# Attention with a gated feed-forward on one core: another hand-written order of TensorE's work, with longer runs of value blocks and the maxima's transpositions inside them

## The chip, the cores and the metric

One NeuronCore of a Trainium2 chip runs the whole program. The metric is the device time of one execution in microseconds (us), as the median of several runs; lower is better. A second source is one profiled execution, whose trace gives every instruction's engine, start and duration. TensorE is called PE here, VectorE DVE, ScalarE ACT, GpSimd POOL and SyncE, which issues most DMAs, SP.

## The reference

A layer norm, a 32-head attention of head width 16 over 2048 tokens, and a SwiGLU feed-forward that gates the attention's output; everything in float32.

```python
def reference(A_x, A_wqkv, A_wo, B_x, B_w1, B_w3, B_w2):
    x = A_x                                    # [1, 2048, 512]
    xn = _layernorm(x, axis=-1)
    s = _A_ref(xn, A_wqkv, A_wo)               # softmax(q k^T / 4) v, 32 heads of 16, then @ wo
    g = _silu(_B_ref(xn, B_w1, B_w3, B_w2))    # (silu(xn w1) * (xn w3)) w2, F = 1792
    return x + s * g
```

## The kernel before

A prologue of about 159 us normalises x, projects it to q, k and v (split into a high and a low part, so that single-pass float32r products keep the precision) and starts on the maxima of the first scores. Then one long main part runs two things at once on PE: the attention, phase by phase (32 phases: 16 pairs of heads times two halves of the queries), and the feed-forward. A tail adds the output projection.

PE's work in the main part consists of four kinds of pieces:

- **Half products** use 64 of the array's 128 rows, so two of them, one on rows 0 to 63 and one on rows 64 to 127, can run side by side. The code calls these two the lanes 0 and 1. There are three sorts: scores (`e`, line 627, one per head of the pair), products for the maxima (`m`, line 389, the scores of a later phase with queries on the partitions, of which only the row maximum is kept), and products of the feed-forward (`f`, line 858).
- **Value blocks** (`pv`, line 640): four matmuls that multiply one tile of keys' exponentials with the values. They use all 128 rows and a quarter of the columns each, and add up in one PSUM bank that belongs to them.
- **Transpositions** of the negated maxima (`m<-ident,nm`, line 404), one a phase. What they give goes by ACT and DVE (`mh`, `ml`) and four small DMAs on SP (line 415) into two extra rows of the query tile `qs`. The first score of that phase needs these rows.
- **Output products** (`o`, lines 195 to 199) near the end.

Every half product ends in one of seven PSUM banks (`take`). A bank comes free when ACT has exponentiated the scores into `pt` (line 630), when DVE has reduced the maximum (line 391), or when ACT or DVE has taken a feed-forward sum. So a bank that is asked back too early makes PE wait, and since PE executes in the order of its program, everything behind waits too.

That order is written out by hand in `ORDER_OF_ISSUE`, a text with one letter for each piece: `s`, `m`, `f` are halves on lane 0 and `S`, `M`, `F` on lane 1; `v` is a value block; `r` forces the next phase's maxima through (reduction, negation, transposition: `second`) and then issues a value block; `R` does the first alone; `o` is a piece of the output projection. A loop at line 1253 reads the letters one by one. A letter that cannot be issued yet by the kernel's own bookkeeping goes to the list `late` and is tried again before the next letter. That bookkeeping (`class Model`, line 231) keeps estimated times: `lane` says when each lane will be free, `free_at` when each bank will be, and they decide which bank `take` gives out, when a chunk of keys may be opened, and when SP's loads are issued. The result is a fixed program; nothing of it is decided on the chip.

A stretch of half products between two interruptions (value blocks, transpositions, output products) is called a stretch below, and consecutive value blocks with the transpositions between them a run.

Of the kernel before, what the change touches and what calls it, by code (L numbers as in the profile page):

```python
# [55 lines left out]
    "FMfFffFMsFfmFSfMfFfsMfFFfSfMfSfmFvmSMmmFmFvvvsMfSfFSffMfFFsfMFsfFsMFfFsmFSffFmSFffSrvsMfMfSFffFsFmFf"
    "SFmsFfFfMsFFmFsFmFfSmvmSfSMsMfvmSMmMsvvfMfSSfMfSffMfSfFfMfFsFmFsFsFmFfFsFmFsFfMfFfSmMfSfsMffSsvmSSff"
    "MsMvsSmSmMvvSfMffSfMfSfSfMfMfFfFmFsFfFfFsMfFfSmSfFfFmFsFmFmFsFfFsFfFmSfFmFsFfFfMfMfMsMvsMfMMsvsMSmFm"
    "vSmmFFmmFmFmFvvvmSmFfFFmsFFfmFsFFfsFfMSfFfMfSfMfMfSfFffMsFFfSfMfSfFfMfsFsRvvSmMffSfSfMffSfSmFfFsFmFs"
    "FFfMfFsFfsMFffSMffSfFmSfFsFMfFfSfmFsFsFmFFfmFsFSffFmMvSmsSmMvsFmSmSmFvvmFSmsMsFvsMFmMssFvsMMmsSvsFmS"  # L60
    "FmmSvSmfFmSfSfFFfmSfFmFsFFffSmFsFfFMsfFSfMffFFsmMvsMMmmFmFvvvsMfSfFMfFffSmSfFmFsFfFMfSfMfFfsMfFFssFr"
    "vvSmfFSfFmfSFfmSfFsFMfsFFfmFSffFMsfFFsMffSFfMffMMfsFFfFfMsfFFmFsFfMfmFsFFfMfmFFfMsvvSmsSSmvmSsMvvMff"
    "SSffFMfFssFmFfFsFMfsFFfMfSfmFsFFffFfMSffMSffSfMfFsFfMsFfFmFsFsFmFfFsFmFmFfSmvmSmSSfvmSmMMsvSmSmvSmSf"
    "FfMffFSfmSFfMfsFfFmFsFFfMfsFmFFmFfMfmMvvvMsMsfFfFFsfFMsfFsFFfmFFssFFfMfSffSsFrvvSfMffSfMSffSfMfMfFfS"
    "fFsFmFfFsFmFsFmFsFfFsMfSfFmMvSmmSmFFsvSmmSMsvMsMfsFsFfFFfMsfFFsmFSffFMsFffMfFMfSfMsvmSMmfSvvMfSsfFmF"
    "FfFsmFFfsFMfSffSmFFffSMfFfSfMmvSmFmmFsFvSmmSMsvSmmFfSSffFfFmSfFsFMfFsfFMsfFFsMffSFfMmvSmFmMmvvSfMffM"
    "fSfSfSfMfFfFsFmFsFfFmSfFsMfFfFmFsFmFmMvvrsMFfsFMfFsFfMsFfsFMfSfFfmSfFmFsFmFfFMfMfmSvvSfMfMffSfSfMfSf"
    "FfMfFsMfFsFfMfFsFfMsFsFfFmFsFfMmFfMfSvSmsMMsvSmmSfMvsMMmSffSvvMffSfMfSfMfSfSfFfFmFsFmFsFfSfMfFsFmSFf"
    "FmSfFsFmFfFsMfMfFsMfFsFFsFfFfMfSfMssFvSmMmFsvSmFsmFmSvSmmMsSvSmFsFsmMvSmmFmFsFFmmFmFvvvMsfSMffSfFfFs"
    "MfFFsMffSFffMsFfSMffMFfSfFfSfsMFfFffSSfsSRvvvsMfMMfSffFFffMsFfFFsfMsFfFMfsFmFSfmFFfSffSfFmFmFsFFmFfs"  # L70
    "FmFFfSffMFfsMvvSmSsMmvSmMmfSvvMfmSFmFsfFfFsFmFFfsFsFmFsFFfmFsFFfMsFfsFMfFsFfmMfFSfSfFmvvSmmSfSFfFfFf"
    "mFfSfMfSFffMsFmFfFsFmFMfmFFfMsvvsMfSsFFmFffFMsFfSfmFFsFfsMFfmFfSFfFsmMvSmmSSfvMssSmMvMsSfMfSmvmSMmSs"
    "vvmSfSSfMfFffFSfMffSSfmFFfsFmFFfFsmFsFfMsFmFsRvvSmFfMfSffMFfMfSffFmFmFsFFfFsMfFffFsFFmMmvsMFmsSvMssS"
    "mMvvmFFssFsMFfFfMffSfFMsfFSfMfsFfFmSFffFfSmSvMmsFfFfFfSFmfSfFSmfFfSmFSffFmSfFmFSfmFfFmMvSmMssFvmSsMM"
    "svmSmFsFfSfFFmsFFfmFSfmFfSFmfFMsFfmMvvsMMssMvMsMsfSMfvvMfSffMMfMffSfMfSffFfFsFmFfFsFsFFmFsFffMsFFfMm"
    "RvSmSfSffMfFfFmSfFfSmFsFfFMsfFmFsFMffFsFSfMmvsMMmmFvvSfmFfSSfmFfFSfmFsFFfmSFfFsmFFsFfMmFffMSfvsMfSMs"
    "vvMfSsFfFmFsfFsFmFfFsFsFMffFmFSffFMfmMvvSfMffSfMSffSfMfSfFfFmFsFmFsFfFsFmFfFsMsFfMmFvsMfSfMmSvSmfSsF"
    "FmfFfFsMFffSmFSfFfMsfFmFsFmFfFMfMfMmvvfSMmMmvvsMFmFsFfFsFfmFsFfFsFMfSfMfSffFfMsFsFMfRvMsfMSffSfSfMSf"
    "vMsMfSfSsvmSSfmMvMsSfSfMsvmSfSFfFmFfFsmFFsmFFfsFFmsFFmFfSffMfMSfFffSMfSffFSfmFsFFfmSfFsFMfMffFmMvsMf"
    "MmMvvmMsMFsFsvsMSmSmvsMFsfFSmFffFmFSfmFfSFffMsFFmfFsMFfSffFFmSfFsMfMfFfsFMffFsFfFMfsSvMfSssMMfvsMmMS"  # L80
    "svSmFmmSvSmmFmMmFvvvmSfFsFmFFsfFSmFfsFFmFsfFSmfFmFmFsFFfsFFmFffMSfMfSffMSfRvsMfMfSMfSffMfSfMfSvSmfMs"
    "FsFFfFfMsFfsFmFFsfFmSfFMfmFsFFfsMvSmmSFfFfsFFfmFSfsFmFmFvvvvmSfFFfsSMffFFfFsmFFsfSfMFfFsFmFmfFmSvSmM"
    "mfMSfvSmSfMsvMsMfsFFfFsFfMsFfsFmFfSfFmSfFfSFmfFmFsSvmSSfMfsMvsMmMMmvvvfSMffSfMSffSFfmFsFFfmSfFsFfFMf"
    "SfsFsFmFFfsFrvMsfMfSfFfSFffMfSFmFsMfFfSfmFfFsFmFFfsFmFmMvsMFfsFFmFsFfsFMfSfSfmFFffSmFSffFmFFmMfvSmMs"
    "SfMfvsMMsSsvmFSmSmvvMffSfMfFsMFffSfMFfsFSfmFSfFfmFfFsFFmFffSMfsFfFFmfFSfmFsFfSmFFfmFSfFmfFSfmFmMvvsM"
    "sMsMvsMMfMsvSfMsFmFsFfFfmFFsFmfFSmFfSfMfFfsFMfMfMfFfMmvvvsMSffSfFfFmFsFfFsFmFFsFffSMfFfSfSmFfSfsFrvv"
    "SmfSfFFfSmfFSmFfSffFSmfFSffMsFFfMfsFmFFmFffMsFfFmFFsfFfSmFfSfFFmsFmFfMFsFfmMvmSfSSmvMsMsMsvsMfMMfSsv"
    "sMMsMsvvMffMSfMffSfFsFfFmFsFmFmFSffFmFsFFfmFMffSvsMSsSmvMfMsfFFssFFfmFFsFfsFmFSffSmFfFfSMffMfFSmvmSM"
    "fsMvSmsSFmmFvSmmSMmvvmSSfSfmFfFFfMsfFFsMfsFfFMsfFMffSsFfFMffMfSSffSfMrMsMsvSmmMsSvvSfMffSSffMfMfMfSf"
    "MfsFfFfFFsFmFsFmsFFfMfsFfMfFMsfFFmSfFffMsFmFFfSfmFfFSfmFfFmSvvSmsSmFFmvSmSmMmvvmFsFMfmFsFFfFsFmFfSff"  # L90
    "MFssFfFMfSffMfSfFfSmFfFsFMsFfFsMfFffMFffSfMSmvvsMmMsMvvSfMfSffMfMfSfMfFsFfFsMfFsFfFsMfFmFsFsFfFmFfSf"
    "MmFfSfSfFmFfSfFmFsFmFfSmFfMmvvMsSssFvrvSmfSSfmFfFfFmSFfFsmFFsFfmFsFsFsFmFfFFfmSFfmFsFFfmFSsfFmMvvSmS"
    "sMmvsMMsSfvmSMsSsvmFSfMfFfsMFfFsmFFfSfmFFfSffMfFsFmFfFMmfMvvMffMfSfSfSfFMffFsFFfMsFfFsmFfFFsmSfFFmmF"
    "vsMMmSfvsMsFFfMfFsFfmSFfSfmFFsfFmSFfmFSfSffFMfmFMmvvSsMsmMvvsMfMfSFffSfMSffMfSfMfFsFsFfMFfsFmFsFmFmF"
    "FmFmFsvvsMfFFmsFfFFmMfsFfFfSFfMsFfSfMfFfSfMfFsMRvvsMMffSSffFFfMsFfSfMfsFfFmFsFFmsFFfmFFmfSmSvSmmSSmv"
    "SmMfsSvMssMSmvsMsFFmFfFfSmSfFfMfSfFmSfFfFmSfmFFsmFfFMmvvMsfSMfsMvMsmSsSvMsFmsFsFfFfFmFSffSmFFsFfMfsF"
    "fFMfmFMffSvsMmSsMvsMfMSfSmvsMfMfMsFfFFfSfmFfFSmfFfSfMFfSffMmFmFvvvvRFsFmFfMffFSffMfFfSfFmFFsfFmSFfSf"
    "mFFsfFmFFffSMffMfSfFsFfFmFsFsFmFsFfSfMfFfMsFfFmFmSvmSsFFfMfFsfFMsFfFsfMFsFfsMfFFmSfFmFfSffSMmvSmsSsM"
    "vMssSMfvmSsMsMvSmfFmSFffSFfmFSfMffSfMFfsFmFFfsFmFmFFmvvMmSfMsSfvSmmMsSvSfMsFfsFMfFfsFmFsFFfMsfFfMsFs"
    "FFfMfFfMfSfMfMfSfMfvsMMsMfMfvSsMmvSmfMMmSfvSfmMMmvvvSmsFFffFmFsFFssFmFFfFfSfmFFssFmFFfSfmFfFSfmFsFfF"  # L100
    "MfsFSfRvvSfMffSSffSMfSffMfMvsMMfSsFfFfFfsMFfFsfMsFFfmSfFFsfMfSFfsMFffFmSfFfMsFfFsFmFFsFfmFFfMffSmMvS"
# [12 lines left out]
    "mFFsmFFfsFFmmFfMfMMfvvvSmfMSffSfMfSffSmFFfsFFmfFFsFmmFsFfFSfFmSfFffMfSRvvSmsFsFFmFffFFmsFFfmSfSFfmFs"
    "FfFmMvsMsMsMvsMMsSfMfvSmMmsSvsSMfSfmMvsMMfMfsFFffFsFMffFsMFfFsFfFmSfmFfSFffFMmvsMMsMsvvMffSfFSfmSfFF"
# [1238 lines left out]
```

## Time and profile before

| what | us |
|---|---|
| median of 3 runs | 1740.31 (1739.88 to 1740.66) |
| profiled execution, span from first to last instruction | 1737.7 |
| PE busy / DVE / ACT / POOL in it | 1730.3 / 1432.1 / 1254.2 / 765.5 |
| 2048 scores' exponentials on ACT (line 630) | 1085.7 busy, 606 ns each |
| 2048 reductions of maxima on DVE (line 391) | 1298.5 busy, 684 ns each |
| 4096 matmul records of the 512 value blocks (line 640) | 508.7 busy, 596 ns each |

The result for the profiled execution is its span; the runs that are timed include 2.6 us more around it (1740.31 against 1737.7). In the rows of the time line each row begins with its start and its length in us; rows of equal instructions that follow each other are merged, with their number at the end (x8). Each float32 matmul of a value block leaves two records, so a block of four matmuls shows as x8. A matmul's end is modelled in this profile and overlaps the next one's, so what PE really needs for a piece is read from start to start.

### The profile page before, as it was taken

The page shows a single profiled execution, that of the slowest core. Times are in us where ns is not written, and L with a number is a line of the kernel's source. Part 1 is how long each engine was busy: PE and PEld are TensorE (multiplying, and loading weights), DVE is VectorE, ACT ScalarE, POOL GpSimd, SP SyncE. Part 2 cuts the span into 40 slices and gives each one's busy share as a digit, 9 for nine tenths or more (in the row PEclk, how much of TensorE's full clock was granted, in tenths as well). Part 3 has the DMA queues.
Part 4 walks back from the last instruction along what each step waited for, and adds up shares of the span by engine and source line. Part 5 has one row for each costly group of instructions (what it writes and reads, how often), then busy time and mean ns, then how long its engine had stood idle before and what let it go on. Part 6 is the DMA issues. An engine that isn't in the chain of part 4 may idle for free.

```text
span 1737.7 us, 35616 instructions
## 1 busy us (share of the span) xinstructions
PE 1730.3 (100%) x13236; PEld 1044.5 (60%) x13236; DVE 1432.1 (82%) x2349; ACT 1254.2 (72%) x2440; POOL 765.5 (44%) x793
## 2 busy tenths in 40 slices
PE   9999999999999999999999999999999999999999
PEld 7877656565665555555655655565655555566456
DVE  7567989888888889789888888888988988888535
ACT  4223787878878787778778877887788777777762
POOL 3103653365535560566265623644455515661201
PEclk9999999999999999999999999999999999999999
DMA  8657213122323121222423221132523222421542
GB/s 288 241 205 206 65 33 68 50 69 63 80 84 91 53 72 28 69 66 75 105 74 68 57 63 52 46 72 56 135 56 68 70 35 55 115 76 37 180 152 97
DMA packets 147373, 155.36 MB, mean 89 GB/s; under 512 B 42368, under 2 KB 101760, under 8 KB 144224
## 3 DMA queue, kind: packets, MB, share of 16 engines
q1 hardware_dynamic: 146336, 152.04, 31.7%
q8 instruction: 104, 1.70, 0.4%
q10 hardware_dynamic: 864, 1.05, 0.2%
q14 instruction: 69, 0.57, 0.1%
HBM read 107.97 MB, written 44.02 MB: 87 GB/s over the span
## 4 chain that ended last, share of the span: by engine, by line
PE 98%; DMA 1%; DVE 1%; SPq 0%; ACT 0%; issue 0%; POOL 0%; POOLq 0%; ACTq 0%
PE f L858 28%; PE pv L640 27%; PE e L627 17%; PE m L389 14%; PE m L507 3%; PE e L195 2%; PE e L199 2%; PE e L197 2%; PE o L195 1%; PE o L199 1%; PE o L197 1%; PE m L480 0%; PE m L404 0%; DMA wl<-g 0%; DMA ovl<-o 0%; PE o L1089 0%
## 5 line engine op out<-in xcount | busy, mean ns | idle before, releaser
L391 DVE TENSOR_REDUCE mp<-m 128x1 f32<-128x512 f32 x2048 | 1298.5, 684 | 164.2 <-PE m L389 89.8
L630 ACT ACTIVATE pt<-e 128x512 f32<-128x512 f32 x2048 | 1085.7, 606 | 268.4 <-PE e L627 121.2
L627 PE MATMUL e<-qs,ks 64*128 64x512 f32 x2048 | 716.0, 411 | 0.0
L389 PE MATMUL m<-ks,qs 62*128 62x512 f32 x2048 | 697.8, 413 | 0.0
L640 PE MATMUL pv<-pt,vt 128*17 128x512 f32 x4096 | 508.7, 596 | 0.0
L627 PEld LDWEIGHTS e<-qs,ks 64*128 64x128 f32 x2048 | 344.6, 185 | 228.7 <-ACT pt L630 85.0
L389 PEld LDWEIGHTS m<-ks,qs 62*128 62x128 f32 x2048 | 334.7, 184 | 141.0 <-ACT pt L630 42.8
L640 PEld LDWEIGHTS pv<-pt,vt 128*17 128x17 f32 x4096 | 84.0, 96 | 206.7 <-issue 199.9
L858 PE MATMUL f<-xth,wh 64*128 64x512 f32 x488 | 171.1, 392 | 0.0
L858 PE MATMUL f<-xth,wl 64*128 64x512 f32 x488 | 170.8, 396 | 0.0
L858 PE MATMUL f<-xtl,wh 64*128 64x512 f32 x488 | 169.7, 392 | 0.0
L743 POOL TENSOR_TENSOR h<-g,h 128x512 f32<-128x512 f32 x56 | 72.0, 1286 | 198.8 <-ACT h L739 198.8
L858 PE MATMUL f<-wh,hs 64*128 64x512 f32 x496 | 157.3, 394 | 0.0
L858 PE MATMUL f<-xth,xel 64*128 64x512 f32 x408 | 146.7, 394 | 0.0
L858 PE MATMUL f<-xth,xeh 64*128 64x512 f32 x408 | 143.1, 393 | 0.0
L858 PE MATMUL f<-xtl,xeh 64*128 64x512 f32 x408 | 142.5, 392 | 0.0
L858 PE MATMUL f<-xeh,hs 64*128 64x512 f32 x400 | 122.7, 393 | 0.0
L322 POOL TENSOR_TENSOR wl<-wr,wh 128x512 fp32r<-128x512 f32 x92 | 118.5, 1288 | 7.7
L322 POOL TENSOR_TENSOR xel<-wr,xeh 128x512 fp32r<-128x512 f32 x76 | 98.0, 1289 | 6.3
L727 POOL TENSOR_SCALAR th<-th 128x512 f32<-128x512 f32 x56 | 34.7, 620 | 143.2 <-ACT th L720 143.0
L321 POOL TENSOR_SCALAR wh<-wr 128x512 fp32r<-128x512 f32 x92 | 57.2, 621 | 86.5 <-PE f L858 85.5
L321 POOL TENSOR_SCALAR xeh<-wr 128x512 fp32r<-128x512 f32 x76 | 47.3, 622 | 101.0 <-PE f L858 48.2
(179 smaller groups left out, 2089.5 us busy)
## 6 DMA issues: line engine op xcount, KB each, us to landing
wr<-in_B_w_dram SPq DMA_DIRECT2D x168, 256.0 KB
qs<-qk SPq DMA_DIRECT2D x186, 64.0 KB
ks<-qk SPq DMA_DIRECT2D x90, 128.0 KB
qk<-sh SPq DMA_DIRECT2D x32, 256.0 KB
qk<-sl SPq DMA_DIRECT2D x32, 256.0 KB
v<-vrow SPq DMA_DIRECT2D x16, 272.0 KB
xin<-in_A_x_dram SPq DMA_DIRECT2D x16, 256.0 KB
g<-part SPq DMA_DIRECT2D x16, 256.0 KB
```

Source lines behind the costliest of these rows:

```text
L195: nc.tensor.matmul(ps, lhs[1], rhs[0], start=first, stop=False)
L197: nc.tensor.matmul(ps, lhs[0], rhs[1], start=False, stop=False)
L199: nc.tensor.matmul(ps, lhs[0], rhs[0], start=False, stop=last)
L321: nc.gpsimd.tensor_scalar(hi, t, 1.0, 1.0, op0=ALU.mult, op1=ALU.mult)
L322: nc.gpsimd.tensor_sub(lo, t, raw(hi))
L389: nc.tensor.matmul(ps, qs[p % 2][64 * h:64 * h + KM, q0:q0 + P], ks[p % 2][64 * h:64 * h + KM, c * 512:(c + 1) * 512], start=True, stop=True)
L391: nc.vector.reduce_max(mp[p, half][:, h, qt, c:c + 1], ps, axis=AX.X)
L627: nc.tensor.matmul(ps, ks[p % 2][64 * h:64 * h + KR, k * P:(k + 1) * P], qs[p % 2][64 * h:64 * h + KR, q0:q0 + 512], start=True, stop=True)
L630: nc.scalar.activation(pt, ps, AF.Exp, scale=DH ** -0.5)
L640: nc.tensor.matmul(pv[32 * j:32 * j + VW, :], vt[2 * p // GH][:, key, 2 * p % GH + j % 2, :], pt, start=key < 2 if last else k == 0, stop= ...
L743: nc.gpsimd.tensor_mul(h2, g, h2)
L858: nc.tensor.matmul(ps, left[r], right[r], start=starts and lane == 0, stop=ends and lane == 1)
```

## The change

The text `ORDER_OF_ISSUE` is replaced by another one, from the first line to the last. It names the same pieces (2016 `f`, 2016 `F`, 1024 `s`, 1024 `S`, 992 `m`, 992 `M`, 512 value blocks and 22 `o`; the other 64 maxima's products belong to the prologue) in another order. `r` now stands 30 times and `R` once; before it was 18 and 13. In the old text 351 runs of the letters `v`, `r`, `R` interrupt the halves, in the new one 276.

The bookkeeping changes in one function. `half` now lets an issue come no earlier than the start of the half before it on the same lane, since PE's instructions go out in order; and it returns the later of the two lanes' last starts, from which `free_at` is counted. This changes which bank is given out and when a late letter is tried, not what is computed.

```diff
 ORDER_OF_ISSUE = (
-    "MffSfMfSfMfSfSfMfSfMfMfSfMfsMsFFfFffFsMMfMfsFFfFfMsfFfFMsfFmFmFvmMmMFsFffFfFfMFsfFFfFffMSfMffFFmFmfS"
-    "vFmfSFmFfmFfFSfFmFmfFfSfFFmFsFfFfMfMffMMsvSfMfsFfFmFsFMffMsFfFfMsFfFsFMfFsfFMfFfMmvSmmSmFFmvSmmSFmvS"
...
+    "MfSfMffSMffSSffMfSffMfSfFFMMfffMMfsFfsFfFSffmFsFFfMsFfMFfmmFFmMFvvSmmFsFfSffMsFfmFFsFfMsfFSfMfFfMsFS"
+    "ffMFfFffMFSfFfMfSfSfmsfFmFFsFmFsFfFmSfmFfFmMfFMmvvFsMMsFsfFfFmFsfFMsfFFmsFmFFfSffMfFfMMfFMfMfMsvvSmf"
...
         def half(self, h, there):
 
             load = max(self.issue, there, self.begun[h], self.clear)
-            self.issue = max(self.issue, there)
+            self.issue = max(self.issue, there, self.begun[h])
             begins = max(load + self.LOAD, self.lane[h])
             self.begun[h], self.lane[h] = begins, begins + self.SLOT
             self.turned = False
-            return begins
+            return max(self.begun)
```

The text has a line less, so a line of the kernel after it carries a number lower by one than before: 640 is now 639, 404 is 403. PE's order is the same up to row 612, which is the beginning of the main part, and another from there to the end. Two places of PE's queue show what moved; in these rows a value block is `17x512 x4`, and two blocks in a row are `x8`.

The first is in the fifth phase's scores, where the values come in quick succession (`e` is a score, `m` a product for a maximum, `f` one of the feed-forward). Before:

```order
L640 MATMUL pv<-pt,vt 17x512 x4
L627 MATMUL e<-qs_133,ks_135 128x512
L389 MATMUL m<-ks_134,qs_132 128x512
L858 MATMUL f<-wl_2822,hs 128x512
L389 MATMUL m<-ks_134,qs_132 128x512 x2
L627 MATMUL e<-qs_133,ks_135 128x512 x2
L858 MATMUL f<-wh_2821,hs 128x512
L640 MATMUL pv<-pt,vt 17x512 x4
L627 MATMUL e<-qs_133,ks_135 128x512
L389 MATMUL m<-ks_134,qs_132 128x512 x3
L627 MATMUL e<-qs_133,ks_135 128x512 x2
L640 MATMUL pv<-pt,vt 17x512 x4
```

And of the change, at about the same place:

```order
L639 MATMUL pv<-pt,vt 17x512 x8
L626 MATMUL e<-qs_133,ks_135 128x512
L388 MATMUL m<-ks_134,qs_132 128x512
L626 MATMUL e<-qs_133,ks_135 128x512 x4
L639 MATMUL pv<-pt,vt 17x512 x8
L626 MATMUL e<-qs_133,ks_135 128x512
L388 MATMUL m<-ks_134,qs_132 128x512
L626 MATMUL e<-qs_133,ks_135 128x512
L388 MATMUL m<-ks_134,qs_132 128x512 x2
L626 MATMUL e<-qs_133,ks_135 128x512
L639 MATMUL pv<-pt,vt 17x512 x4
```

Three runs held three blocks before; here three runs hold five.

The second is the fourth transposition of negated maxima on PE (`m<-ident,nm`). Before:

```order
L627 MATMUL e<-qs_133,ks_135 128x512
L858 MATMUL f<-xeh,hs 128x512
L627 MATMUL e<-qs_133,ks_135 128x512
L404 MATMUL m<-ident,nm 16x128
L640 MATMUL pv<-pt,vt 17x512 x8
L627 MATMUL e<-qs_133,ks_135 128x512
```

And of the change:

```order
L388 MATMUL m<-ks_134,qs_132 128x512 x3
L639 MATMUL pv<-pt,vt 17x512 x4
L403 MATMUL m<-ident,nm 16x128
L639 MATMUL pv<-pt,vt 17x512 x4
L857 MATMUL f<-xel,hs 128x512
```

The transposition stood at the head of its run; now a value block goes ahead of it and one follows it.

More of the change, by code (lines that the diff above doesn't have):

```diff
@@ L56 @@
[L56 to L65, printed above, removed]
@@ new lines @@
+    "FsFfmFmFsFMsvvMsMmSsvFmsFMmmSvvmSSfMfFfSffMSffFmFFsSfmFFmFfsFfFSffMFmMmvvMsSffFfMfSfMfSFfmFFsmFfSfFF"
+    "msFFsfFFsFmsMvvsMSmMsvMmfMSfmMFvvMFssfMffSfMfSFfmSFffSmfFsFFmSfFFmsFfFFffMfSfMffSMfFFsmFfFmfSfFSfFmF"
+    "sfFFmFsfSFsFmvrvvMsSffMFfSffMSffFmSSFffFmsFffMFSffMsFfsFMfFmFFfsmFmMvFvsMsMMsvMmsMfFSSfvSmMsMsvSmffS"
+    "MffSFfMfSfMffSmsfFmSFfSfmsFfFSmFfFFmFsFmfSsFFfmFfSFfmFsFmSfFMfFffFmMMmvvMsfMfSMsvMssMMsvmSFfMsFsfFFm"
+    "fFSmFsFfmFFsFfMsfFsFmFSfFfMfFsfSmFsFfFMfSffFMsFfMfFffMfMMffMMmvvvSmmMSmvvSmmSFfSffFFmsFFmFsFfFmSfSfF"
@@ new lines @@
+    "mfFfMSsfFFmfSfFmFsFFmFsfFFmSffFsFMffMMmvrfMFMsMmMfvvvfMSfMfSffSfMffSfMFsfmFFsFmSfsFfFFmfFmSfFFsFmFsF"
+    "fmFsFFmsFFFmFssFSsvvSmsSsSvvSmSmmSvmSFmsFFfFsFmfSFfMsfFfSFmfSfFMfSfSfFmfMFfFFmMvvsMsMsfFfFmFfMsfFsFM"
+    "ffSfFMfSfFmSfFsFfFfmMMsvrsMMssMvMsSfMffSFffMFfmSfSFfmFFsFfmFsFfMsFfFfFmSFmmMvvmSsMMmvvsMsFFmFmFsFfFs"
+    "fFSmfFSfMfFfSfMffSfFSmfFFffFFMSffMfFSffSmfsMfsFFmFsFmFsFmFfFMfmFMmvvMsMmfSfSvmSsMSmvMsfMfSfFSffMFfmS"
+    "fSFfFmFfsFmsFfFSFmfSfFmfFfFMSFfffFSFmsFfmFFmsFfsFSffMFFffmFFfMmMmvvvvmMSsMsvSmsFmFmFFsFsFfFfSmFfSfMf"
@@ new lines @@
+    "FffMSffFsMfFfFMffSFfFMfSfSfFMfsmsFfFmsFfFMsFmFfSfmFfFFmfMMmvvvmSMssSvrvSmmFsFsFmFFsfFFfMsfFfMfSfFfMS"
+    "mfFfSfFfMFsfMFMsvvvmFsFmsFFmsFFffSfMfSFfmSfFmFsFMffFSfSfMmvmSMffMsSvsMSfSffMFfFfSmfFsFMfsFfFsMFfFmsF"
+    "sFfMFfffFMfSffSFMffMsfSFfFmFsfFMsfFmFsFFfFmFmFmSmvvvSmsSsSvvSsMmMsvfSfMSfMfSffMfSfFfSfMFfsFFsmFfsFMf"
+    "sFfFMsFfmFSFfffMFMfssMvsFSFMmMsvrvMsfSMfffSfMSffMFffSmssfFMFfsFmfFsFFmfSFmfFSffSFmSFfFmsFFfmFsFfMsFM"
+    "fFffSmFSmvvSmMsMmvvmMSfmSSfvSmmSMsvSmsFFmsFFfFmSffFSmfFSfMfSffFMsfFMfsFFfMfsFfFsMFffSMfSffFsMFfmFFsm"
@@ L138 @@
+    "MomSMsSSMSvMsSsMSmvsMMSsmSvMsMsSsvMssSMsoSSsSsvvsMsSsMMvSsSsSsMvvSoMmSSsvMssMSmSvSmSSmsMvSmsSmsMMvSv"
+    "vSRososSoSsosSSsSsvvsSSsSsoosSsSsSvvvvSsSssSosSSssSvvosSSsoosSSsoooosoSvvSsSsSsvvSssSSsooosSsSovvvv"
 )
```

142 lines of the change are left out of this document (67 added, 75 removed).

## The prediction

> **What bounds the kernel now.** I read the page first, then the chain of waits, the stages, and PE's time line around the places that the change moves.
>
> ```profile
> PE 1730.3 (100%) x13236; PEld 1044.5 (60%) x13236; DVE 1432.1 (82%) x2349; ACT 1254.2 (72%) x2440; POOL 765.5 (44%) x793
> PEclk9999999999999999999999999999999999999999
> PE 98%; DMA 1%; DVE 1%; SPq 0%; ACT 0%; issue 0%; POOL 0%; POOLq 0%; ACTq 0%
> ```
>
> PE is the bound from end to end: it fills the span, 98% of the chain that ended last is its own, and the granted clock is full throughout. By stage:
>
> ```profile
> 0.00:159.40 159.40, 157.50 (x733) 122.69 (x733) 105.20 (x188) 45.29 (x93) 32.10 (x44) 1.00 0.70 239
> 159.40:1613.90 1454.50, 1454.50 (x11759) 852.52 (x11762) 1267.59 (x2062) 1141.53 (x2213) 721.10 (x736) 1.00 0.27 69
> 1613.90:1717.70 103.80, 102.10 (x629) 54.37 (x621) 47.70 (x77) 66.02 (x131) 6.08 (x7) 1.00 0.47 149
> 1717.70:1737.70 20.00, 16.15 (x128) 14.96 (x120) 11.61 (x23) 1.32 (x3) 6.26 (x7) 1.00 0.32 111
> ```
>
> The columns are span, then busy time of PE, weight loads, DVE, ACT and POOL. The first 159.4 us keep their order and the last 20 have no text behind them; the change acts on the 1558 us between, where DVE is at 87% (1267.59 of 1454.50) and ACT at 78%. But a busy PE can still be slow, since overlapping ends hide pauses, so I take PE from start to start.
>
> **What a run costs.** The first row pair is two halves, one on each lane, then a run of one block; the next group is a run of three, the last a run of one near the end.
>
> ```profile
> 217.66 0.39 PE L627 MATMUL e<-qs,ks 64*128 64x512 f32 x1
> 217.89 0.39 PE L627 MATMUL e<-qs,ks 64*128 64x512 f32 x1
> 218.22 1.05 PE L640 MATMUL pv<-pt,vt 128*17 128x512 f32 x8
> 219.20 0.50 PE L627 MATMUL e<-qs,ks 64*128 64x512 f32 x2
> 219.54 0.39 PE L389 MATMUL m<-ks,qs 62*128 62x512 f32 x1
> 220.33 1.05 PE L640 MATMUL pv<-pt,vt 128*17 128x512 f32 x8
> ...
> 1201.91 2.77 PE L640 MATMUL pv<-pt,vt 128*17 128x512 f32 x24
> 1204.61 0.50 PE L389 MATMUL m<-ks,qs 62*128 62x512 f32 x1
> ...
> 1580.30 0.39 PE L627 MATMUL e<-qs,ks 64*128 64x512 f32 x1
> 1580.62 1.05 PE L640 MATMUL pv<-pt,vt 128*17 128x512 f32 x8
> 1581.60 0.50 PE L627 MATMUL e<-qs,ks 64*128 64x512 f32 x1
> 1581.94 0.39 PE L858 MATMUL f<-wh,hs 64*128 64x512 f32 x1
> ```
>
> A pair of halves takes 0.23 us (217.66 to 217.89). From the run's first matmul to the next half are 0.98 us with one block and 2.70 with three, so a block is (2.70 - 0.98) / 2 = 0.86. With one block it is 1.31 us from the last half to the next (217.89 to 219.20), and the pair behind takes 0.34 instead of 0.23. So a run costs, beside its blocks, 1.31 - 0.23 - 0.86 + 0.34 - 0.23 = 0.33; the late run gives 1.30 and 0.34, hence 0.32. It is the same at every length and whichever work stands beside it, so PE's own turn sets it and not a wait. I take 0.32.
>
> **The change part by part.** All counts are from the two orders of PE's instructions as built, from the first feed-forward product on.
>
> Fewer runs: halves are interrupted 357 times before (350 by runs, 7 by output products alone) and 278 times in the change (270 and 8). Runs of a single block go from 225 to 100. That is 79 x 0.32 = **-25.3 us**.
>
> Transpositions inside runs: 6 before, 29 in the change.
>
> ```profile
> 304.76 0.39 PE L627 MATMUL e<-qs,ks 64*128 64x512 f32 x1
> 305.09 0.28 PE L404 MATMUL m<-ident,nm 128*16 128x128 f32 x1
> 305.29 1.91 PE L640 MATMUL pv<-pt,vt 128*17 128x512 f32 x16
> 307.13 0.49 PE L627 MATMUL e<-qs,ks 64*128 64x512 f32 x1
> ...
> 871.60 1.05 PE L640 MATMUL pv<-pt,vt 128*17 128x512 f32 x8
> 872.58 0.28 PE L404 MATMUL m<-ident,nm 128*16 128x128 f32 x1
> 872.79 1.91 PE L640 MATMUL pv<-pt,vt 128*17 128x512 f32 x16
> ```
>
> At the head of a run it adds its 0.20 (305.09 to 305.29); behind a block the block first takes 0.98 (871.60 to 872.58), 0.12 over its 0.86. So 23 x 0.12 = **+2.8**. In exchange PE need not wait there for the negation, but at 304.76 to 305.09 it enters the run in the usual 0.33: nothing is gained, because nothing was waited for.
>
> Uneven lanes: the old text nearly always puts as many halves on one lane as on the other. Summed over the stretches, the longer lane has 4053 halves before and 4073 in the change: 20 x 0.23 = **+4.6**.
>
> Halves out of step: the old text has no lane letter three times in a row, and in 13 stretches only is a half issued while its lane is two or more behind the other; in the change in 66. Here is one such stretch of 77 halves (39 on one lane), and one of 66 (33 and 33) without:
>
> ```profile
> 831.40 0.49 PE L627 MATMUL e<-qs,ks 64*128 64x512 f32 x1
> 840.79 1.05 PE L640 MATMUL pv<-pt,vt 128*17 128x512 f32 x8
> ...
> 847.50 0.50 PE L389 MATMUL m<-ks,qs 62*128 62x512 f32 x1
> 855.36 1.05 PE L640 MATMUL pv<-pt,vt 128*17 128x512 f32 x8
> ```
>
> At 0.2325 a pair, 0.10 for the slow first pair and 0.32 into the run, they should take 38 x 0.2325 + 0.42 = 9.26 and 32 x 0.2325 + 0.42 = 7.86; they took 9.39 and 7.86. So being out of step for a while cost 0.13 there, but other stretches in step lose as much. Below it can be nothing, above 53 x 0.14 = 7.4; I take **+2**, nearer to nothing.
>
> In a sentence of its own: the Trainium skill ("TensorE: Matmul & The Clock Gate", the step on LDWEIGHTS) says that PE's queue pulls a weight load ahead of running matmuls where the row groups don't conflict, while matmuls keep their order; by that a load for the other lane need not stand behind one that waits, and this term would be 0 and the sum 2 lower, where the row of 9.39 shows at least a little.
>
> Tighter handovers: how soon is a bank asked back?
>
> ```profile
> 307.13 0.49 PE L627 MATMUL e<-qs,ks 64*128 64x512 f32 x1
> 307.14 0.73 PE L389 MATMUL m<-ks,qs 62*128 62x512 f32 x2
> 307.66 0.60 ACT L630 ACTIVATE pt<-e 128x512 f32<-128x512 f32 x1 [0.96 <-PE m L389]
> 307.70 0.69 DVE L391 TENSOR_REDUCE mp<-m 128x1 f32<-128x512 f32 x1 [0.68 <-PE m L389]
> ```
>
> From a matmul's start to the end of its exponential are 0.53 + 0.60 = 1.13 us (307.13 to 308.26), to the end of its maximum 1.25. Places where a bank is retaken within 1.2 us of its matmul, at the paces above, number 89 before and 145 in the change. Each of the 56 more can wait between nothing and about 0.1: 0 to 5.6, and I take **+2**. DVE keeps a rate of 0.60 us when it is never idle (here 20 maxima in 12.02 us),
>
> ```profile
> 286.15 12.02 DVE L391 TENSOR_REDUCE mp<-m 128x1 f32<-128x512 f32 x20
> ```
>
> and where the change is densest, three maxima (1.80 us) come with every six halves and a block. Seven halves and a block take 2.11 us above (218.22 to 220.33), with a pair less 1.88. It just fits.
>
> The rows for the next phase: a score waits for what the transposition sends off.
>
> ```profile
> 306.73 0.71 SPq L415 DMA_DIRECT2D qs<-mh  x1
> 308.93 0.63 SPq L415 DMA_DIRECT2D qs<-ml  x1
> ...
> 1399.81 0.35 SPq L656 DMA_DIRECT2D rd<-rec  x1
> 1401.24 1.70 SPq L659 DMA_DIRECT2D rb<-rd  x4
> ```
>
> The transposition at 305.09 has its fourth DMA issued at 308.93, and a small DMA lands no later than 1.43 us after its issue (the second pair: the later one reads what the earlier one wrote), so the rows are there about 5.3 us after the transposition. Before, the first score on lane 1 never comes sooner than 6.5 us behind it; in the change it comes within 6 us in six phases, at the least 5.3. Each of these can lose between nothing and one DMA's issue, 0.7: 0 to 4.2, and I take **+1**.
>
> What PE takes from POOL and from larger loads I cost at nothing, since halves and blocks of about 6 us hide it: the nearest such use stands 5.9 us behind the PE work that it needs, 6.1 before, at eight places in all; if the old distance was just enough, that is 8 x 0.2 = 1.6 us.
>
> The sum is -25.3 + 2.8 + 4.6 + 2 + 2 + 1 = **-12.9** us. The span goes from 1737.7 to 1724.8; with the 2.6 us around it that the median of the runs has (1740.31), 1727.4.
>
> **The rivals.**
> - *Only the countable terms act.* The last three terms are nil, because ACT, DVE and the queue absorb them as they do now: -25.3 + 2.8 + 4.6 = -17.9, **1722.4**. For it: stretches like 847.50 that run to the hundredth. Against: the 9.39.
> - *The lanes out of step eat the gain.* A third half in a row on one lane cannot load its weights before the second has begun, and the other lane's next half stands behind it. 550 halves are issued while their lane is two or more behind, 147 before; at 0.032 us for each of the 403 more they cost another 13 us and nothing is left: **1740**. Against it: the stretch at 831.40 has 16 such halves and lost 0.13, 0.008 each.
> - *Value blocks wait for the last exponentials.* With blocks in longer runs more of them come soon after their scores: 59 value blocks carry a wait for ACT of their own instead of 32, the nearest 1.85 us behind the last score instead of 2.27. If ACT is one exponential further behind (0.60) at each of the 59, that is 35 us, and the time is 1727.4 + 35 = **1762**; it decides from 0.22 us each, where 12.9 is used up. Against it: 1.85 is well over 1.13, and now runs are entered in 0.33 us, without a wait.
>
> **How the numbers follow.** The sum 0.52, only the countable terms 0.28, the gain eaten 0.11, value blocks late 0.09. No change means within 0.2%, 3.5 us, about what a measurement of this kernel can tell. Faster by more is the first two, 0.80; the same 0.11; slower 0.09. The first case alone reaches from -17.9 (its last three terms nil) to -17.9 + 13 = -5 (three quarters of their upper bounds, 7.4 + 5.6 + 4.2 = 17.2), 1722 to 1735. The range goes a little below the second case and stops short of the third: 1720.5 to 1737.5.
>
> **What would show it.** In the changed profile a run of one block should still take 1.31 us from half to half, and 270 runs should stand where 350 did; the value blocks' 439 us (512 x 0.86) are the same. Stretches should run at 0.23 a pair; one that pauses in mid-stretch with DVE or ACT as the releaser shows the handovers, a longer pace where a lane is ahead shows the out-of-step term, more than 0.33 into a run the third rival. Wrong would be the forecast if the last value block, now at 1717.7, began later than about 1713.

## The result, and the profile after

| | before | after |
|---|---|---|
| median of the runs, us | 1740.1 (4 runs) | **1723.77** (1722.71 to 1724.77, 4 runs) |
| ratio to before | 1 | **0.9905** [0.9891, 0.9919] |
| span of the profiled execution, us | 1737.7 | 1723.0 |
| from the first feed-forward product to the last value block, us | 159.4 to 1717.7 | 160.4 to 1702.4 |

The kernel is 16.3 us faster. In the profiled executions the main part, which the text orders, takes 1542.0 us instead of 1558.3, 16.3 less; the prologue is 1.0 longer and the end 0.6, which no line of the change touches.

The page of the profile after (busy time, granted clock, and the engines' shares of the chain that ended last):

```profile
PE 1715.4 (100%) x13236; PEld 1099.0 (64%) x13236; DVE 1418.7 (82%) x2349; ACT 1240.6 (72%) x2440; POOL 766.5 (44%) x793
PEclk9999999999999999999999999999999999999999
PE 98%; DVE 1%; DMA 0%; issue 0%; POOL 0%; ACT 0%; SPq 0%; DVEq 0%; ACTq 0%; POOLq 0%
```

PE still fills the span, with the same 13236 records, at full clock but for the last 20 us, where it is 0.96. Everything that was gained is PE's own time. By stage (span; then busy PE, weight loads, DVE, ACT, POOL, each with its count; clock; DMA):

```profile
159.40:1613.90 1454.50, 1454.44 (x11849) 913.45 (x11847) 1257.02 (x2069) 1139.29 (x2235) 721.70 (x736) 1.00 0.28 70
1613.90:1703.00 89.10, 88.51 (x541) 48.68 (x540) 43.76 (x70) 54.63 (x110) 6.13 (x6) 1.00 0.45 152
1703.00:1723.00 20.00, 15.58 (x120) 14.86 (x120) 11.61 (x23) 1.33 (x3) 6.28 (x7) 0.96 0.33 119
```

The first row is the same stretch of time as before, 1454.50 us. PE is busy in both, but 11849 matmul records fit in it, where 11759 did: a busy PE says nothing here, the count does. At 1454.5 / 11759 = 0.124 us a record the 90 more are worth some 11 us, by this estimate most of the gain. The second row, from there to the last value block, has shrunk from 103.8 to 89.1 us and holds 88 records less.

A run of one block, and a run with a transposition inside, on PE's time line (start, length, instruction, number of merged ones):

```profile
541.12 0.39 PE L626 MATMUL e<-qs,ks 64*128 64x512 f32 x1
541.44 1.05 PE L639 MATMUL pv<-pt,vt 128*17 128x512 f32 x8
542.42 0.28 PE L403 MATMUL m<-ident,nm 128*16 128x128 f32 x1
542.63 1.05 PE L639 MATMUL pv<-pt,vt 128*17 128x512 f32 x8
543.61 0.50 PE L626 MATMUL e<-qs,ks 64*128 64x512 f32 x1
543.95 0.39 PE L857 MATMUL f<-xth,xel 64*128 64x512 f32 x1
...
1579.57 0.39 PE L626 MATMUL e<-qs,ks 64*128 64x512 f32 x1
1579.89 1.05 PE L639 MATMUL pv<-pt,vt 128*17 128x512 f32 x8
1580.87 0.50 PE L626 MATMUL e<-qs,ks 64*128 64x512 f32 x1
```

One block takes 1.30 us from half to half (1579.57 to 1580.87), as before. Over all runs of a kind the medians of before and after agree to 0.003 us: 1.307 and 1.308 with one block, 2.165 and 2.167 with two, 3.024 and 3.025 with three. PE enters the run in 0.32 (541.12 to 541.44), and the first pair behind takes 0.34. The transposition stands between two blocks of 0.98, 0.21 after its own start: 0.12 more than at the head of a run, as put down in the prediction, and without a wait. So the prices of the prediction hold to the hundredth, and what differs is how often they are paid.

The groups that hand banks back and ask for them (busy us, mean ns; then idle us before them and what ended it):

```profile
L390 DVE TENSOR_REDUCE mp<-m 128x1 f32<-128x512 f32 x2048 | 1287.1, 683 | 204.3 <-PE m L388 130.0 <-PE e L626 53.9 <-PE f L857 9.1
L629 ACT ACTIVATE pt<-e 128x512 f32<-128x512 f32 x2048 | 1072.3, 606 | 280.0 <-PE e L626 161.2 <-PE m L388 101.0 <-PE f L857 7.2
L626 PE MATMUL e<-qs,ks 64*128 64x512 f32 x2048 | 709.0, 408 | 0.6 <-DMA qs<-ml 0.5
```

DVE and ACT have the same work in less time. The last row holds what the scores wait for the next phase's rows: 0.5 us in the whole execution, once, at 1646 us.

Below, a stretch's *excess* is what it takes over its own pace, from its first half to its last: (halves of the longer lane - 1) x 0.2325 + 0.104 for the slow first pair. Summed over the main part, it is 9.4 us before (356 stretches) and 11.9 after (277).

### The profile page after: what moved, and what is told of

The parts are those of the page before. It is cut to its first block, busy times and chain, and to the rows that moved or that the text cites. A ratio compares the mean times of both kernels' runs of the same rounds, so it can differ in the third digit from the quotient of the medians.

```text
span 1723.0 us, 35685 instructions
## 1 busy us (share of the span) xinstructions
PE 1715.4 (100%) x13236; PEld 1099.0 (64%) x13236; DVE 1418.7 (82%) x2349; ACT 1240.6 (72%) x2440; POOL 766.5 (44%) x793
## 4 chain that ended last, share of the span: by engine, by line
PE 98%; DVE 1%; DMA 0%; issue 0%; POOL 0%; ACT 0%; SPq 0%; DVEq 0%; ACTq 0%; POOLq 0%
PE f L857 28%; PE pv L639 28%; PE m L388 16%; PE e L626 16%; PE m L506 2%; PE e L194 2%; PE e L198 2%; PE e L196 2%; PE o L194 1%; PE o L198 1%; PE o L196 1%; PE m L479 0%; PE m L403 0%; DMA qs<-ml 0%; PE o L1088 0%; DVE wr L1035 0%
## 5 line engine op out<-in xcount | busy, mean ns | idle before, releaser
L629 ACT ACTIVATE pt<-e 128x512 f32<-128x512 f32 x2048 | 1072.3, 606 | 280.0 <-PE e L626 161.2
L388 PE MATMUL m<-ks,qs 62*128 62x512 f32 x2048 | 708.2, 416 | 0.1
L639 PE MATMUL pv<-pt,vt 128*17 128x512 f32 x4096 | 497.4, 595 | 0.0
L639 PEld LDWEIGHTS pv<-pt,vt 128*17 128x17 f32 x4096 | 90.2, 96 | 220.0 <-issue 210.2
L857 PE MATMUL f<-xtl,wh 64*128 64x512 f32 x488 | 174.6, 392 | 0.0
L857 PE MATMUL f<-xtl,xeh 64*128 64x512 f32 x408 | 148.9, 392 | 0.0
L857 PEld LDWEIGHTS f<-xth,wl 64*128 64x128 f32 x488 | 85.4, 185 | 7.3 <-issue 3.4
L857 PEld LDWEIGHTS f<-xth,wh 64*128 64x128 f32 x488 | 86.9, 185 | 4.9 <-issue 0.8
```

What stands on the lines that cost most here:

```text
L388: nc.tensor.matmul(ps, qs[p % 2][64 * h:64 * h + KM, q0:q0 + P], ks[p % 2][64 * h:64 * h + KM, c * 512:(c + 1) * 512], start=True, stop=True)
L629: nc.scalar.activation(pt, ps, AF.Exp, scale=DH ** -0.5)
L639: nc.tensor.matmul(pv[32 * j:32 * j + VW, :], vt[2 * p // GH][:, key, 2 * p % GH + j % 2, :], pt, start=key < 2 if last else k == 0, stop= ...
L857: nc.tensor.matmul(ps, left[r], right[r], start=starts and lane == 0, stop=ends and lane == 1)
```

## The experiments

Twelve kernels, all on the same question: which part of the new order carries the gain, and what do lanes out of step, transpositions and handovers of banks cost? Medians in us; "after" is 1723.77.

| kernel | median | ratio to before |
|---|---|---|
| old text, new bookkeeping | 1739.54 | 0.9996 [0.9987, 1.0006] |
| new text, old bookkeeping | 1723.5 | 0.9905 [0.989, 0.992] |
| after, 79 runs split | 1748.34 | 1.0047 [1.0032, 1.0062] |
| after, transpositions at the end of their run | 1727.42 | 0.9926 [0.9913, 0.9938] |
| after, transpositions at the head | 1728.39 | 0.9931 [0.9917, 0.9944] |
| after, lanes alternating singly | 1742.62 | 1.0015 [1.0006, 1.0025] |
| after, lanes alternating by twos | 1789.5 | 1.0284 [1.027, 1.0298] |
| after, lanes alternating by threes | 1842.2 | 1.0587 [1.0572, 1.0601] |
| after, short maxima and exponentials | 1710.26 | 0.9828 [0.9814, 0.9843] |
| before, the same shortening | 1729.12 | 0.9937 [0.9922, 0.9952] |
| single alternation, the same | 1713.76 | 0.9849 [0.9832, 0.9865] |
| alternation by twos, the same | 1727.19 | 0.9926 [0.9911, 0.9941] |

### The text or the bookkeeping

The old text with the new `half`:

```diff
-            self.issue = max(self.issue, there)
+            self.issue = max(self.issue, there, self.begun[h])
...
-            return begins
+            return max(self.begun)
```

> The old order text with the new bookkeeping of half(). Theory A (the time is counted in pieces: 0.32 us for each interruption of the halves, 0.23 a pair, 0.86 a block): the text alone carries the gain, so this stays at 1740, within 3 us. Rival B (the bookkeeping carries it, because banks are given out and late letters tried at truer times): about 1724 to 1730.

Measured 1739.54: no change. The reverse, the new text with the two lines as they were:

> The new order text with the old bookkeeping of half(). Theory A: 1724, within 3 us. Rival B: near 1740.

Measured 1723.5, as fast as the change (1723.77). So the whole gain is the order; the bookkeeping, which picks banks, carries nothing by itself in either order.

### The price of a run

In the changed order the last value block of 79 runs is moved behind the next pair of halves, which makes 356 interruptions out of 277:

```diff
-... mmFFmMvvSmFmFsFf ...
+... mmFFmMvSmvFmFsFf ...
```

(The row of the change is its order as built, in which a late letter stands where it was issued; so it is below for the lanes.)

> The changed kernel, with the last value block of 79 runs moved behind the next pair of halves (one on each lane), so that the halves are interrupted as often as before (357 times); the pieces are the same. Theory A: 79 x 0.32 = 25 us and 4 more uneven slots, 1 us: 1750, between 1746 and 1754. Rival C (a run's cost is a pause that covers waits for banks which come anyway, so that cutting runs only moves waits): less than half of that, under 1736.

Measured 1748.34, 24.6 us slower than the change. The longer lanes have 4 halves more (0.9 us), which leaves 23.6 / 79 = 0.30 us for a run. Counted start to start in the two traces, the waits in and ahead of the stretches are 1.3 us less here than in the change and the groups with output products 0.6 less, which makes up the difference to 79 x 0.32 = 25.3. So the price of 0.32, read off PE's time line, is the price of a run on the chip, and the 79 fewer runs of the change are worth about the 25 us that the prediction gave them.

### Where the transposition stands

The 29 transpositions inside a run moved to the end of their run (`R` is a transposition without a block, `r` one with a block behind it):

```diff
-FmFsfSFsFmvrvvMsSffMFfSf
+FmFsfSFsFmvvvvRMsSffMFfSf
```

> The changed order, with the 29 transpositions of negated maxima that stand inside a run of value blocks moved to the end of their run, behind its last block (nothing else moves). Theory: what a transposition inside a run costs is that it parts two blocks: a block takes 0.98 us before it where it takes 0.86 before another block. At the end of the run the last block takes its 0.98 anyway, so 29 x 0.12 = 3.6 us are saved; the next phase's rows are ready about 1 us later, which can give back up to 6 x 0.7 us. Span 1723.0 -> 1719.4 to 1721; time 1720 to 1722, ratio to before 0.9885 to 0.9897. Rival: the price belongs to the change between a block's column quarters and the transposition's whole array, wherever they meet; then nothing is saved, 1723.8 to 1725.

Measured 1727.42, 3.65 us slower than the change, where 2 to 4 less were expected. PE's time line of this kernel at the run that is shown above:

```profile
542.66 0.39 PE L389 MATMUL m<-ks,qs 62*128 62x512 f32 x1
542.99 1.91 PE L640 MATMUL pv<-pt,vt 128*17 128x512 f32 x16
544.83 0.28 PE L404 MATMUL m<-ident,nm 128*16 128x128 f32 x1
545.04 0.49 PE L389 MATMUL m<-ks,qs 62*128 62x512 f32 x1
```

The run itself is cheaper, as the theory had it: 2.38 us from half to half (542.66 to 545.04), where inside the run it takes 2.49 (541.12 to 543.61). By medians of two-block runs that is 2.375 against 2.499, some 3.5 us over the 29. But the stretches' excess rises from 11.9 to 18.6 us. The time line of all engines behind another such run shows why:

```profile
259.86 0.28 PE L404 MATMUL m<-ident,nm 128*16 128x128 f32 x1
260.18 0.25 ACT L407 CAST mh<-m 16x128 fp32r<-16x128 f32 x1 [1.92 <-PE m L404]
260.46 0.28 DVE L408 TENSOR_TENSOR ml<-m,mh 16x128 fp32r<-16x128 f32 x1 [3.36 <-ACT mh L407]
260.63 3.46 ACT L630 ACTIVATE pt<-e 128x512 f32<-128x512 f32 x6 [0.20 <-PE e L627]
260.67 4.01 DVE L391 TENSOR_REDUCE mp<-m 128x1 f32<-128x512 f32 x6
...
262.26 0.18 PEld L627 LDWEIGHTS e<-qs,ks 64*128 64x128 f32 x1 [0.27 <-ACT pt L630]
```

The copy on ACT and the subtraction on DVE that make the rows now fall on the first halves of the next stretch, and the transposition's bank is taken then; 2.4 us after the transposition a load waits 0.27 for an exponential's bank, and this stretch exceeds its pace by 0.77, where in the change it does so by nothing. In the change the same two operations start at 258.19 and 258.48, while PE is at value blocks that need no bank of the seven. The late rows that the expectation feared were not it, since in this kernel one score waits for a DMA, for 0.12 us; what came back was bank handovers.

The same 29 at the head of their run:

```diff
-FmFsfSFsFmvrvvMsSffMFfSf
+FmFsfSFsFmRvvvvMsSffMFfSf
```

> The changed order, with the same 29 transpositions at the head of their runs, as most stood before the change. By the trace of the changed kernel the negation is done before the run's first matmul in 27 of the 29 (by 0.1 to 20 us), and 0.1 and 0.6 us after it in two. Theory (as in the prediction: at the head nothing is waited for, inside a run it costs 0.12 more): 29 x 0.12 = 3.5 us less and 0.8 lost at the two, time 1721, ratio 0.989. Rival (the negation is what a block has to go ahead of; the chip is less punctual than one trace): no gain or a loss of up to 29 x 0.3 us, 1724 to 1732.

Measured 1728.39, 4.6 us slower than the change: the theory falls, and the rival's price is right but not its reason. What PE and its loads waited for ahead of the 32 transpositions in this kernel (us in all, times; loads and matmuls count apart):

```profile
  DVE mp L391: 9.8, 21
  ACT pt L630: 9.3, 22
  ACT nm L400: 2.9, 4
```

The negation (`nm`) is last in four rows only. Elsewhere it is `mp` and `pt`, a maximum and an exponential: the transposition needs a bank like any half, and at the head of the run it asks for one right behind the last halves. The waits that the program has for each transposition, matched with the times at which the semaphores were set in the trace, agree: 25 of the 32 start at the moment that their wait ends, 23 of them with a bank and 2 with the negation; in the change none of the 32 does. PE enters a two-block run in 0.67 there (median) instead of 0.32. With a block of 0.98 us ahead, the bank is free in the meantime. So the block that goes ahead in the new text covers a bank, not the negation, which in the change is done 6.4 us before the transposition (median). In the order before, 24 transpositions stood at the head of a run and were entered in 0.32 (median), since that text put them where a bank was free; put at the head of the new text's runs, they are not.

### Lanes out of step

Three kernels put the halves of every stretch alternately on the lanes, one by one, by twos and by threes, each lane keeping its own sequence, the runs where they are. The text of the second stretch in the change and in the three:

```diff
-vvSmFmFsFfSffMsFfmFFsFfMsfFS
+vvSmFmFsFfSfMfFsFfFmFsMfFsSf
...
+vvSFmmFFsfSMffFFsfFFmsMFfsSM
...
+vvSFFmmsFSMfffFFFsfmFMFsfsSM
```

> The changed kernel with each stretch's halves in another order: one of lane 0, one of lane 1 in turn, each lane keeping its own sequence. Halves issued while their lane is two or more behind go from 550 to 45; runs, slots and transpositions are unchanged. Theory A with the price read before the change (0.008 us each): 4 us less at most, 1720 to 1724. Rival D (in-order issue is dear, 0.03 us each or more): 15 us less, 1708 or below. If the tighter handovers of banks matter more than the lanes, it could also be slower by some us.

Measured 1742.62 with 45 halves issued while their lane is two or more behind, instead of 550: 18.9 us slower, the whole gain lost; neither theory A nor rival D allowed for that, only the sentence on handovers. Prices of runs are unchanged, and the excess of the stretches goes from 11.9 to 30.8 us. In step is worse than out of step. (How many halves are out of step depends on how they are counted. Taken from the orders as built, with every half before which the other lane was given at least two more since the last run, they are 167 before, 577 in the change, and 51, 1895 and 2560 in the three kernels here; the smaller counts, 147 and 550 among them, were put down before the runs, and nothing turns on the difference.) The same stretch on PE's time line, in the change:

```profile
274.84 0.39 PE L857 MATMUL f<-xel,hs 64*128 64x512 f32 x1
274.84 0.40 PE L388 MATMUL m<-ks,qs 62*128 62x512 f32 x1
275.07 0.39 PE L857 MATMUL f<-xeh,hs 64*128 64x512 f32 x1
275.08 0.40 PE L626 MATMUL e<-qs,ks 64*128 64x512 f32 x1
275.29 0.39 PE L857 MATMUL f<-wh,hs 64*128 64x512 f32 x1
275.45 0.49 PE L388 MATMUL m<-ks,qs 62*128 62x512 f32 x1
275.52 0.39 PE L857 MATMUL f<-wl,hs 64*128 64x512 f32 x1
```

and with single alternation:

```profile
277.09 0.40 PE L389 MATMUL m<-ks,qs 62*128 62x512 f32 x1
277.09 0.39 PE L858 MATMUL f<-xel,hs 64*128 64x512 f32 x1
277.32 0.39 PE L858 MATMUL f<-xeh,hs 64*128 64x512 f32 x1
277.33 0.39 PE L627 MATMUL e<-qs,ks 64*128 64x512 f32 x1
277.56 0.39 PE L389 MATMUL m<-ks,qs 62*128 62x512 f32 x1
277.70 0.50 PE L858 MATMUL f<-wh,hs 64*128 64x512 f32 x1
277.83 0.50 PE L627 MATMUL e<-qs,ks 64*128 64x512 f32 x1
278.04 0.40 PE L858 MATMUL f<-wl,hs 64*128 64x512 f32 x1
```

and there the loads of its last three rows:

```profile
277.70 0.18 PEld L858 LDWEIGHTS f<-wh,hs 64*128 64x128 f32 x1 [0.18 <-ACT pt L630]
277.83 0.18 PEld L627 LDWEIGHTS e<-qs,ks 64*128 64x128 f32 x1
277.83 0.18 PEld L858 LDWEIGHTS f<-wl,hs 64*128 64x128 f32 x1
```

One lane has feed-forward products (`f`) only, the other scores and maxima in turn, faster than their banks come back. In the change the second lane pauses (275.08 to 275.45), and the first goes on every 0.23 (275.07, 275.29, 275.52), since its halves stand in the program ahead of the one that waits. With single alternation the halves of both lanes stand in turn, and both pause (277.32 to 277.70 on the one, 277.56 to 277.83 on the other). These two pauses are each lane's own: the `f` at 277.70 begins a new sum and waits for a bank from ACT, set free at 277.65, and the `e` for one from DVE, set free at 277.79 (both times are those of the semaphores). What one lane does to the other shows in the row behind: the `f` at 278.04 needs no bank, but stands in the program behind the `e`, is loaded with it at 277.83 and starts 0.34 after the `f` before it, not 0.23. That suggested that a lane ahead is a buffer, and that more of it would be better:

> The changed order with the halves of each stretch put alternately by twos (two of lane 0, two of lane 1, and so on; each lane keeps its own sequence, and the runs stay where they are). Halves issued while their lane is two or more behind: 550 in the changed kernel, 45 when they alternate singly (which took 1742.6), 1633 here. Theory (a lane that is ahead is a buffer: its halves stand in the queue before the one that waits for its bank, so the array has work): better than single alternation, 1727 to 1736, and no cost at all for the 1633. Rival 1 (each half issued out of step costs about 0.03 us): 1723.8 + 1083 x 0.03 = 1756 or more. Rival 2 (what was lost with single alternation is only that its order of banks is not the hand-found one): about the same 1742 again.

> As the one by twos, but alternating by threes: 2031 halves are issued while their lane is two or more behind, 975 of them three or more. Buffer theory: as good as by twos or better, 1723 to 1732. Rival 1 (0.03 us each, more where a lane is three behind): 1768 or more. Rival 2 (only the order of banks was lost): about 1742.

Measured 1789.5 and 1842.2: neither. Both are far slower, 66 and 118 us above the change, all of it in the stretches (excess 78.7 and 130.7 us). It looks like a price for each half out of step: 0.06 us for the 1083 more. But in the kernel by twos whole pieces of a stretch run at full pace:

```profile
702.60 0.39 PE L627 MATMUL e<-qs,ks 64*128 64x512 f32 x1
702.71 0.39 PE L858 MATMUL f<-xth,xel 64*128 64x512 f32 x1
702.84 0.39 PE L858 MATMUL f<-wh,hs 64*128 64x512 f32 x1
702.94 0.39 PE L627 MATMUL e<-qs,ks 64*128 64x512 f32 x1
703.07 0.39 PE L858 MATMUL f<-wl,hs 64*128 64x512 f32 x1
703.17 0.39 PE L389 MATMUL m<-ks,qs 62*128 62x512 f32 x1
703.30 0.39 PE L858 MATMUL f<-wh,hs 64*128 64x512 f32 x1
703.40 0.39 PE L858 MATMUL f<-xtl,xeh 64*128 64x512 f32 x1
```

Each lane takes 0.23 a half here (702.60, 702.84, 703.07, 703.30; 702.71, 702.94, 703.17, 703.40), out of step as they are. What the two kernels have more of must be something else, and the last group asks whether it is the banks.

### Handovers of banks

In four kernels every maximum is taken over 256 of its 512 columns and every exponential over 256, which leaves out half of that work; the value blocks read those columns twice, so that PE's work, its order and the choice of banks stay (the exponential's scale is made smaller too, since a maximum over half of the columns does not bound the rest).

```diff
-        nc.vector.reduce_max(mp[p, half][:, h, qt, c:c + 1], ps, axis=AX.X)
+        nc.vector.reduce_max(mp[p, half][:, h, qt, c:c + 1], ps[:, :256], axis=AX.X)
...
-        nc.scalar.activation(pt, ps, AF.Exp, scale=DH ** -0.5)
+        nc.scalar.activation(pt[:, :256], ps[:, :256], AF.Exp, scale=DH ** -3)
...
-                             vt[2 * p // GH][:, key, 2 * p % GH + j % 2, :], pt,
+                             vt[2 * p // GH][:, key, 2 * p % GH + j % 2, :], pt[:, None, :256].to_broadcast([P, 2, 256]),
```

> The changed order with every maximum taken over 256 of its 512 columns and every exponential over 256 of its 512 (the value blocks read those 256 columns twice, so that PE's work is the same; the result is not the reference's). PE's order and the choice of banks stay as built. Banks then come free sooner, about 0.25 us after their matmul for each of the two engines, and the two engines keep up at any place. What goes is all that PE loses to handovers of banks. In the changed kernel the stretches of halves exceed their pace by 11.9 us in all and the entries into runs by 3; theory of the handovers: 6 to 12 us of these 15 go, time 1712 to 1718. If the excess is PE's own (lanes out of step): 1720 to 1724.

> The order before with the same shortened maxima and exponentials. Its stretches exceed their pace by 9.4 us. Handovers: 4 to 8 us go, time 1732 to 1736, and the gap to the changed order grows by 1 to 4 us beyond the 16.3 measured: that growth is what the handovers cost in the change. If the gap stays within 1 us, the prediction's +2 for handovers was nothing.

The groups of the shortened change:

```profile
L390 DVE TENSOR_REDUCE mp<-m 128x1 f32<-128x256 f32 x2048 | 811.6, 422 | 627.9 <-PE m L388 382.1 <-PE e L626 156.7 <-PE f L857 67.2
L629 ACT ACTIVATE pt<-e 128x256 f32<-128x256 f32 x2048 | 726.3, 386 | 565.5 <-PE e L626 340.0 <-PE m L388 130.8 <-PE f L857 44.5
```

Maxima take 422 ns instead of 683, exponentials 386 instead of 606, and a value block's matmul record has 596 ns, about as before the shortening (595); a run of one block takes 1.307 us (median), as before it. The change comes to 1710.26, 13.5 us less; its excess falls from 11.9 to 2.3 us, and the mean entry into a run from 0.01 above its median to nothing. That is what the changed kernel loses to waits for ACT and DVE, banks above all, and a little more than was expected. The order before comes to 1729.12, 11.0 us less and also below what was expected, with an excess of 2.7 instead of 9.4. So the gap between the two orders grows from 16.3 to 18.9 us: handovers cost the change 2.5 us more than they cost the order before, or 3.4 by the main parts of the four profiled executions (1558.3 and 1542.0; shortened, 1547.6 and 1527.9).

The excess of 2.3 us is what 277 stretches have left, with 550 halves out of step, and 2.7 is what 356 have with 147. In these two orders, where banks come in time, out of step costs nothing that shows.

> Single alternation of the lanes (1742.6, 18.9 above the changed kernel) with the shortened maxima and exponentials. If its loss is handovers of banks at which both lanes stop: within 3 us of the changed order with the same shortening. If single alternation is slow in itself: still 15 or more above it.

> Alternation by twos (1789.5, 65.7 above the changed kernel; 1633 halves issued while their lane is two or more behind instead of 550) with the shortened maxima and exponentials. If a half issued out of step costs by itself (0.06 us each, by that run): still 55 or more above the changed order with the same shortening. If being out of step is free and only makes each wait for a bank stop both lanes for longer: within 6 us of it.

Measured 1713.76 and 1727.19, 3.5 and 16.9 us above the shortened change; 3.5 is just over the 3 that the theory allowed. Of the 18.9 us that single alternation loses, 15.4 go with the shortening, and so are handovers; of the 65.7 that alternation by twos loses, 48.8. Neither order is slow in itself to the extent that the count of halves out of step would have it (0.06 us each is 65). The 16.9 us that are left by twos are more than the 6 that the theory allowed. They sit in a few stretches (10.9 of an excess of 19.7 us in 21 of 277), which speaks for waits and against a price for each half, but the shortened kernel still has waits for banks, and what part of the 16.9 is not one stays open. That the loads of one lane are held up behind a waiting half of the other can be told from the traces. Take a half that waits for a semaphore, and the half of the other lane right behind it in the program; where the lane and the semaphores of the second were ready more than 0.06 us before the first one's wait ended, the second could have gone first. By twos there are 304 such places, and in 303 of them the second is loaded no sooner than the first; with single alternation it is 241 of 242, in the change 132 of 137. The halves so held start late by 19.4 us in all by twos (both lanes summed), by 5.7 with single alternation and by 1.7 in the change. Fewer halves wait by twos than in the change, about 1410 against 1690, but the waits cost more. Why they do, with the same sequence on each lane, stays open.

## Why the prediction was right, and where its terms were off

The forecast was 1727.4, the measured time 1723.77, in the range and nearest to the second case (only the countable terms act, 1722.4). Term by term:

- **Fewer runs, -25.3.** Right. The price is the same after, and splitting 79 runs gives 24.6 back. (The rows at 217.66 and 217.89, from which the 0.23 was read, are two halves of one lane and not one on each; a product for a maximum starts beside each on the other lane, so 0.23 is the time of a pair all the same.)
- **Transpositions inside runs, +2.8.** Right in size: 0.12 to 0.13 each, 3.2 in all. The sentence that nothing is gained in exchange holds against the order before, where the heads had a free bank. It does not hold for the new text: at the head they would cost 0.3 each for a bank, and at the end 0.2 each in the stretch behind (6.7 us of excess over 29).
- **Uneven lanes, +4.6.** Right as far as it can be told: the stretches' own pace, with these 20 halves in it, is what remains when banks come in time (excess 2.3 us over 277 stretches).
- **Halves out of step, +2.** Nothing: 550 of them leave no trace in the shortened change. The 0.13 us of the stretch at 831.40, on which the term rested, was not theirs: with the shortening the same stretch, in the same order, exceeds its pace by 0.02. By the Trainium skill ("TensorE: Matmul & The Clock Gate", the step on LDWEIGHTS), which has loads pulled ahead where row groups don't conflict, the term was 0, and the run agrees with the size. It does not agree with the reason that the prediction took from it, that a load need not stand behind one that waits: in 132 of the 137 places of the change where a load on the other lane could have gone first, it stood behind.
- **Tighter handovers, +2.** Right: 2.5 by the medians of the shortened pair. Start to start in the two traces all waits for banks and exponentials grew by somewhat more, 2.5 in the stretches (9.4 to 11.9) and 2.0 at the runs of value blocks.
- **Rows for the next phase, +1.** 0.5 in all, one wait near the end. The others arrive in time.

With these, -25.3 + 2.8 + 4.6 + 2.5 + 0.5 = -14.9, where the main part became 16.3 us shorter. The rest lies in a term that the prediction did not have. Groups in which output products stand are 17 before and 12 in the change, with the same 180 products. Beyond 0.86 a block and the 0.45 that any run of value blocks takes over its blocks, they take 45.0 us before and 41.6 after, 3.4 less (2.9 less in the shortened pair). The prediction counted these groups as interruptions at 0.32 and put their inside at nothing. With them the two traces divide up without a rest: -25.3 + 4.6 for runs and lanes, 3.2 for transpositions, 2.5 + 2.0 for waits, -3.4 for the output products, together -16.4. What makes the twelve groups cheaper was not tested.

So the mechanism and its prices held, and what the sum missed in the main part, 3.4 us, is a term that it left out. That the time is nearest to the case without the last three terms is chance: they came, at about 4.5 of the 5 us put down, and the output products hid them. Of the rivals, the second (lanes out of step eat the gain) had the wrong mechanism: the change's out-of-step halves cost nothing, though the two kernels by twos and threes show how dear a careless order of the same halves is. The third (value blocks wait for the last exponentials) did not come: runs are entered in 0.32, and without the shortening the mean is 0.01 above that.

## What to carry to other kernels

Where one engine fills the span, count how often it changes the kind of its work and read the price of a change from start to start; here 0.3 us for each run of value blocks carried more than the whole gain, and its product with the count, 25.3, was right to about a microsecond (24.6 came back). Before an order is rearranged for a reason of its own (lanes in step, a cheaper place for an instruction), ask whose buffers its instructions take: three such rearrangements that looked free or better cost 4, 5 and 19 us, through waits for PSUM banks. Shortening the consumers while the order stays is a cheap way to see how much of a time is such waits.

## What the runs showed of the hardware

Matmuls on different row groups do not start in the order of the program. In the kernel by twos the program has, at the place shown above:

```
L858 MATMUL f<-xth,xel 128x512
L627 MATMUL e<-qs_133,ks_135 128x512
L858 MATMUL f<-wh_8724,hs 128x512
L627 MATMUL e<-qs_133,ks_135 128x512
L389 MATMUL m<-ks_134,qs_132 128x512
L858 MATMUL f<-wl_8725,hs 128x512
```

and on the chip the first `e` starts at 702.60, ahead of the `f` before it at 702.71, and the `f<-wl` at 703.07, ahead of the `m` before it at 703.17; the loads of the weights swap in the same way. So each lane has its own pace of 0.23 us, a little way ahead of the other in the program. A half that waits for a bank is not passed so: what stands behind it on the other lane is loaded no sooner than it, in 303 of 304 places of this kernel (the `f` at 278.04 with single alternation is one such place), while halves ahead of it go on. The Trainium skill ("TensorE: Matmul & The Clock Gate", the step on LDWEIGHTS) says that only the loads are pulled ahead and the matmuls themselves stay in program order; these rows, with 64-row halves on two row groups, show starts out of order by 0.1 us.
